# Eight edits to the order of a sliding-window attention and SwiGLU kernel: transposes of x 6 and 7, weights 10 and 11, scores 8 and 9

## The chip, the core and the metric

The kernel runs on one core of one Trainium2 chip. A core has five engines with instruction queues of their own: TensorE (PE in the profile; PEld is its weight load), VectorE (DVE), ScalarE (ACT), GpSimd (POOL) and SyncE (SP). [...] SP, ACT and POOL issue DMA transfers, which 16 DMA engines of the core carry out. The on-chip memory SBUF holds tiles of 128 partitions; TensorE writes to PSUM, eight banks of 128 x 512 float32, from which VectorE and ScalarE move the results on.

The metric is device time in microseconds, from one execution to another; 325.63 us is the median of three executions of the kernel before. Beside them there is one profiled execution, from which every row below comes.

## What is computed

Causal attention with a window of 64 positions over 8 batches, 8 heads, 576 positions and 64 features, and then, per token, a feed-forward block (512 to 1536 to 512) with a gate:

```python
scores = (1 / sqrt(64)) * q @ k.transpose(0, 1, 3, 2)
mask = (rel >= 0) & (rel < 64)  # rel: query position less key position
attn = softmax(where(mask, scores, -1e9))
x = (attn @ v).transpose(0, 2, 1, 3).reshape(B * S, H * D)
g = x @ w_gate
out = (g * sigmoid(g) * (x @ w_val)) @ w_out
```

Inputs and output are float32; the kernel computes in bfloat16 with sums in float32.

## The kernel before

The 4608 tokens are taken as 36 chunks of 128 for the attention, and as 9 blocks c of 512 for the feed-forward part, so that block c needs chunks 4c to 4c + 3. The program is written out as one list of operations in `build` (L1057). Each names the tiles that it reads and writes, and a small graph (L40 to L140) turns that into semaphore waits. The order of the list is the order in each engine's queue, and each queue runs strictly in that order. What follows names the parts that the change and the prediction touch.

Loads. `load` (L309) brings k, q or v of one chunk from DRAM and casts it; `load2(st)` (L327) brings k and q of two chunks, 2st and 2st + 1, into one of two row buffers (st modulo 2), so that load2(5) has to wait until the transposes of load2(3) have read theirs. `W(a, b)` (L994) brings the slices a to b - 1 of the gate weights and the value weights, 128 columns each. All of these are issued by POOL. `early_loads` (L1019), `more_loads`, `late_loads` and `next_loads` (L1040) group them; next_loads holds load2(5), k and q of 12 and 13 and v of 10 and 11.

Transposes of k and q. `T64(st)` (L371) transposes k and q of chunks 2st and 2st + 1 on TensorE, 64 instructions into two PSUM banks, and returns `ev(x, u, eng)`, which copies k or q of one of the two chunks to SBUF on the engine named. From chunk 12 on, `T` and `Tkq` (L360, L1053) do it by a DMA transpose on SP's queue.

Attention. `S2(n)` (L770) computes the scores of chunks n and n + 1: the products on TensorE, four exponentials on ACT, two masks on DVE. Scores of chunk n need k of n - 1 and n and q of n. `AVw(n)` (L625) multiplies with v for two chunks and divides by the sums; its last step on DVE (L661) writes x of the chunk, `xb`. `B2(n)` (L785) does scores n + 2, n + 3 and the values of n, n + 1 in one piece, in the steady part of the program.

Transposes of x. `X(n, eng)` (L797) brings xb of a chunk into xT, the operand of the feed-forward products. With eng "sp" it is one DMA transpose on SP's queue; with "act" or "dve" it is four transposes on TensorE into a bank and a copy by that engine (`Xp`, L810).

Feed-forward. `F(c, fs, lo, hi)` (L924) computes slices fs of the hidden layer for the tokens lo to hi of block c: four matmuls per slice with the gate weights, tanh on ACT, four per slice with the value weights, then two operations on DVE, `uu` (L902) and `hT` (L904). It takes either one slice for 512 tokens, which is 8 matmuls 512 wide, or two slices for 256 tokens, which is 16 matmuls 256 wide; both fill one bank for the gate and one for the value. `side` takes both banks as a neighbouring pair. `mid` runs something between the gate and the value matmuls. `lastF` is the last matmul group so far, and loads given it as a gate wait for that.

Output. `O(c, u, mid)` (L938) multiplies the hidden layer of 128 tokens of block c with w_out in 12 matmuls, slices 0 to 11 in order, copies the result on ACT and stores it; with `mid` it does nine matmuls, then mid, then three. Each group waits for all the hT slices that it reads before its first matmul. O2 copies on DVE, O3 does six and six.

The bank for a new piece of work is chosen when the list is written: the one, of those not held, whose last use stands furthest back in the list (L225).

Of the kernel before, what the change touches and what calls it, by code (L numbers as in the profile page):

```python
# [153 lines left out]
class _Kernel:  # L154
# [642 lines left out]
    def X(self, n, eng="sp", kind="f"):  # L797
        if n >= NCH:
            return
        g = self.g  # L800
        ix, it, u = n % 4, (n // 4) % self.NX, n % 4
        xb = self.xb[ix]
        xo = self.xT[it][:, :, 128 * u:128 * u + 128]
        xk = [("xb", ix, 0), ("xb", ix, 1)]
        if eng == "sp":
            g.op("sp", lambda e: e.dma_start_transpose(xo, xb[:, :]), reads=xk, writes=[("xT", it, u)], dma=True)
            return
        self.Xp(n, kind)(eng)
# [115 lines left out]
    def F(self, c, fs, lo=0, hi=512, mid=None, side=False):  # L924
        do = self.Fp(c, fs, lo, hi, side)
        for a in range(len(fs)):
            do("Wg", a)
        if mid:
            mid()
        do("tan", 0)  # L930
        for a in range(len(fs)):
            do("Wv", a)
        do("end", 0)
# [4 lines left out]
    def O(self, c, u, mid=None):  # L938
        io = (4 * c + u) % self.NO
        self.Omm(c, u, 0, 512, "act", [("ost", io), ("osth", io)], mid=mid)  # L940
        self.store(c, u)
# [77 lines left out]
    def early_loads(self):  # L1019
        self.load2(2)  # L1020
        self.W(8, 10)
        self.load(4, "v")
        self.load(5, "v")
        self.load2(3)
        self.W(10, 12)

    def more_loads(self):
        self.load_wo(0, 6)
# [28 lines left out]
    def build(self):  # L1057
        F, S, AV, X, O = self.F, self.S, self.AV, self.X, self.O
# [64 lines left out]
        ev = self.T64(2)  # L1123
# [3 lines left out]
        self.late_loads()  # L1127
        F(0, (7,))
        self.S2(4)
        F(0, (8,))  # L1130
        F(0, (9,), side=True)
        self.AVw(4)
        ev = self.T64(3)
        self.next_loads()
        for u in range(2):
            ev("k", u, "act")
            ev("q", u, "act")
        F(0, (10,))
        X(4, "act")
        F(0, (11,), mid=lambda: X(5, "act"))  # L1140
        F(1, (0, 1), 0, 256)
        self.S2(6)
        F(1, (2, 3), 0, 256)
# [2 lines left out]
        self.halves(7, "dve")  # L1146
        F(1, (4, 5), 0, 256)
        self.AVw(6)
        ev = self.T64(4)
        for u in range(2):  # L1150
            ev("k", u, "act")
            ev("q", u, "act")

        def mid():
            X(6, "act")
            X(7, "dve")

        O(0, 1, mid)
        F(1, (8,))
        self.init_kmask()  # L1160
        self.S2(8)
        ev = self.T64(5)
# [2 lines left out]
            ev("q", u, "act")  # L1165
        for n in (12, 13):
            self.Tkq(n)
        F(1, (9,))
        F(1, (0, 1), 256, 512)
        self.O2(0, 2)  # L1170
        self.B2(8)
# [1 line left out]
        X(8)  # L1173
        X(9)
        F(1, (2, 3), 256, 512)
        F(1, (6,))
        for n in (14, 15):
            self.load(n, "kq", self.lastF)
        F(1, (4, 5), 256, 512)
        self.O2(0, 3)  # L1180
        self.B2(10)
        self.store(0, 3)
        F(1, (7,))
        self.T(14, "k")
        X(10)
        X(11)
        self.T(14, "q")
        self.Tkq(15)
        F(1, (10,))
        F(1, (11,))  # L1190
        for n in (12, 13):
            self.load(n, "v", self.lastF)
        for n in (16, 17, 18):
# [84 lines left out]
```

## Time and profile before

| | us |
|---|---|
| median of three executions | 325.63 (324.99 to 326.03) |
| the profiled execution | 325.44 |
| its span, first to last instruction | 323.7 |
| granted TensorE clock | 1.0 of full speed |

| engine | busy us in the span |
|---|---|
| DVE | 218.7 |
| ACT | 127.1 |
| POOL | 104.3 |

A row of a timeline reads: start in us, us that it took, engine, line, operation, what it writes <- what it reads, sizes, how many were merged, and in brackets the idle time of the engine ahead of it and what ended that. An engine with a q behind its name is the sequencer issuing a DMA. In the chain of waits a row has start, us, engine, tile and line. A matmul's own duration in a timeline is longer than its step in a row of matmuls, because they overlap in the array; the chain and the distance of starts give the step. DMA rows give who issued, how many, their size and the median us from issue to landing.

The stretch that the change touches lies between about 27 and 80 us. Before it the kernel fills its pipeline, behind it the blocks 2 to 8 run in a steady order.

### The profile page before, as it was taken

To read this page: it belongs to the slowest core of one execution; us is meant where nothing else is said; L and a number is where in the kernel's file an instruction comes from. 1 tells how busy PE (TensorE), PEld (TensorE's weight loads), DVE (VectorE), ACT (ScalarE), POOL (GpSimd) and SP (SyncE) were. 2 spreads that over 40 slices of the span, in tenths; PEclk is the share of its full clock that TensorE was granted. 3 is DMA by queue.
4 is the path that set the end of the run, shared out by engine and by line. 5 is a ranking of instruction groups with operands and counts; after the bars stand their busy time and mean duration, and the time that the engine had idled before them with its cause. 6 is when DMAs were issued, how large, how long until landed. Compare 5 with 4: busy or idle time off the path is not lost.

```text
span 323.7 us, 7935 instructions
## 1 busy us (share of the span) xinstructions
PE 318.3 (98%) x3390; PEld 163.5 (51%) x3390; DVE 218.7 (68%) x407; ACT 127.1 (39%) x229; POOL 104.3 (32%) x135
## 2 busy tenths in 40 slices
PE   7999999999999999999999999999999999999996
PEld 5654575664545454545454544445454544444444
DVE  6788886678576976766767585858586767555510
ACT  3836656633433432433333332424242422222311
POOL 6998950042626071507060607060402000000000
PEclk9999999999999999999999999999999999999999
DMA  7999999999999699959996999999877202000012
GB/s 188 178 200 191 204 184 189 135 93 129 159 192 129 124 110 143 155 115 138 108 123 123 142 137 87 136 143 150 85 98 104 68 32 67 32 34 32 32 65 99
DMA packets 145219, 39.33 MB, mean 121 GB/s; under 512 B 130208, under 2 KB 140192, under 8 KB 145184
## 3 DMA queue, kind: packets, MB, share of 16 engines
q0 software_dynamic: 97936, 18.36, 69.6%
q1 hardware_dynamic: 41776, 10.63, 23.4%
q10 hardware_dynamic: 5472, 9.83, 9.2%
q8 instruction: 27, 0.44, 0.6%
q14 instruction: 8, 0.07, 0.1%
HBM read 37.75 MB, written 9.44 MB: 146 GB/s over the span
## 4 chain that ended last, share of the span: by engine, by line
PE 93%; POOL 2%; DVE 1%; DMA 1%; ACT 1%; issue 0%; ACTq 0%; POOLq 0%
PE ps L916 57%; PE ps L963 29%; PE ps L727 2%; PE ps L519 2%; DMA hT<-in_q_dram 1%; PE ps L469 1%; POOL vs L256 1%; PE ps L383 1%; ACT pt L481 1%; POOL va L325 1%; POOL Wv L345 0%; PE ps L819 0%; POOL Wg L345 0%; PE ps L473 0%; DVE uu L902 0%
## 5 line engine op out<-in xcount | busy, mean ns | idle before, releaser
L902 DVE SCALAR_TENSOR_TENSOR uu<-sig,ps 128x512 bf16<-128x512 bf16 x108 | 73.8, 683 | 55.9 <-ACT sig L897 55.9
L916 PE MATMUL ps<-xT,Wv 128*128 128x512 bf16 (+1 forms) x464 | 110.9, 364 | 0.3 <-DVE xb L661 0.3
L916 PE MATMUL ps<-xT,Wg 128*128 128x512 bf16 (+1 forms) x464 | 111.1, 365 | 0.0
L897 ACT ACTIVATE sig<-ps 128x512 bf16<-128x512 f32 x108 | 65.0, 603 | 86.7 <-PE ps L916 86.7
L963 PE MATMUL ps<-Wo,hT 128*128 128x512 bf16 (+1 forms) x444 | 98.8, 373 | 0.0
L904 DVE SCALAR_TENSOR_TENSOR hT<-uu,ps 128x512 bf16<-128x512 bf16 x108 | 74.2, 687 | 3.7
L916 PEld LDWEIGHTS ps<-xT,Wv 128*128 128x128 bf16 x464 | 45.3, 98 | 48.2 <-DVE xb L661 0.8
L963 PEld LDWEIGHTS ps<-Wo,hT 128*128 128x128 bf16 x444 | 43.3, 98 | 49.0
L916 PEld LDWEIGHTS ps<-xT,Wg 128*128 128x128 bf16 x464 | 43.6, 98 | 45.1 <-DVE xT L256 0.4
L325 POOL DMA_DIRECT2D kn<-in_k_dram x27 | 23.0, 855 | 113.2 <-PE ps L916 113.2
L325 POOL DMA_DIRECT2D va<-in_v_dram x40 | 34.1, 876 | 24.7 <-PE ps L916 24.7
L255 ACT ACTIVATE ost<-ps 128x512 f32<-128x512 f32 (+1 forms) x22 | 12.9, 588 | 52.9 <-PE ps L963 52.9
L256 DVE COPY ost<-ps 128x512 f32<-128x512 f32 (+1 forms) x15 | 10.1, 674 | 29.7 <-PE ps L963 29.6
L529 ACT ACTIVATE pt<-ps 128x512 bf16<-128x512 f32 x36 | 18.6, 602 | 29.0 <-PE ps L519 29.0
L325 POOL DMA_DIRECT2D qn<-in_q_dram x27 | 23.1, 861 | 2.1 <-DMA Wo<-in_moe_w_out_dram 2.1
L481 ACT ACTIVATE pt<-ps 128x512 bf16<-128x512 f32 x28 | 14.5, 602 | 14.1 <-PE ps L473 14.1
L762 DVE TENSOR_TENSOR xb<-ps,rc 128x512 bf16<-128x512 f32 (+2 forms) x39 | 18.8, 509 | 0.5
L727 PE MATMUL ps<-va,pt 64*64 64x65 bf16 x800 | 12.2, 192 | 0.0
L495 DVE TENSOR_TENSOR pt<-pt,kmask 128x1024 bf16<-128x1024 bf16 x18 | 11.5, 681 | 0.0
L727 PEld LDWEIGHTS ps<-va,pt 64*64 64x64 bf16 x800 | 10.3, 107 | 0.0
L495 DVE TENSOR_TENSOR pt<-pt,mask 128x1024 bf16<-128x1024 bf16 x14 | 9.3, 689 | 1.3 <-ACT pt L481 1.1
L758 DVE RECIPROCAL rc<-ps 128x8 f32<-128x8 f32 (+2 forms) x39 | 5.7, 174 | 6.4 <-PE ps L727 6.4
(76 smaller groups left out, 142.2 us busy)
## 6 DMA issues: line engine op xcount, KB each, us to landing
out_dram<-ost ACTq DMA_DIRECT2D x35, 256.0 KB, 3.0
va<-in_v_dram POOLq DMA_DIRECT2D x32, 128.0 KB, 5.1
kn<-in_k_dram POOLq DMA_DIRECT2D x21, 128.0 KB, 3.8
qn<-in_q_dram POOLq DMA_DIRECT2D x21, 128.0 KB, 4.5
Wv<-in_moe_w_val_dram POOLq DMA_DIRECT2D x6, 256.0 KB, 8.1
Wo<-in_moe_w_out_dram POOLq DMA_DIRECT2D x2, 768.0 KB, 17.7
Wg<-in_moe_w_gate_dram POOLq DMA_DIRECT2D x4, 256.0 KB, 7.8
ks<-in_k_dram POOLq DMA_DIRECT2D x3, 256.0 KB, 9.4
```

The lines of the kernel that those rows point to most:

```text
L256: return self.g.op(eng, lambda e: e.tensor_copy(d, a), reads=reads, writes=writes, after=after)
L325: self.g.op("pool", lambda e, d=d, a=a: e.dma_start(d, a), writes=ks, dma=True, after=gate)
L481: g.op("act", lambda e, po=po, p=p: e.activation(po, sv[p], ACTF.Exp, scale=SCALE), reads=[bx[p][1]], writes=[pk[p]])
L495: self.g.op("dve", lambda e: e.tensor_tensor(pt, pt, m, ALU.mult), reads=pk + mk, writes=pk)
L529: g.op("act", lambda e, po=po, p=p: e.activation(po, sv[p], ACTF.Exp, scale=SCALE), reads=[bx[p][1]], writes=[pk[p]])
L727: x = e.matmul(o, ab[0], ab[1], start=first, stop=phase == 1, skip_group_check=True)
L762: g.op("dve", lambda e, av=av, hs=hs, w=w, rc=rc, xo=xo: e.tensor_tensor(xo[:, :, hs, :], av[:, :, :, 0:64], rc[:, :, hs].unsqueeze(3).to_ ...
L897: g.op("act", lambda e: e.activation(sig[:, 0:w], G[:, 0:w], ACTF.Tanh, scale=0.5), reads=[gk], writes=[("sig", i)])
L902: g.op("dve", lambda e: e.scalar_tensor_tensor(uu[:, 0:w], sig[:, 0:w], 1.0, G[:, 0:w], ALU.add, ALU.mult), reads=[("sig", i), gk], writes ...
L904: g.op("dve", lambda e: e.scalar_tensor_tensor(out, v3(uu), 0.5, v3(V), ALU.mult, ALU.mult), reads=[("uu", i), vk], writes=[("hT", ih, f) ...
L916: r = e.matmul(bank[:, a * n:a * n + n], W[:, kk, f * 128:f * 128 + 128], xT[:, kk, lo:hi], start=(kk == 0), stop=(kk == NK - 1))
L963: r = e.matmul(OB[:, 0:n], hT[:, f, 128 * u:128 * u + 128], self.Wo[:, f, lo:hi], start=(f == 0), stop=(f == NF - 1))
```

## The change

It touches one method of loads and the middle of `build`. Weights 10 and 11 are loaded ahead of k and q of 6 and 7. F(0, 8) and F(0, 9) are done as two halves of the tokens, both slices at a time. T64(3) with its copies and next_loads goes from ahead of F(0, 10) to behind F(0, 11), and two of its four copies go from ACT to DVE. X(6) and X(7) become DMA transposes, issued ahead of T64(4); O(0, 1) runs in one piece. F(1, 6) to F(1, 11), one slice each for 512 tokens, become pairs of slices for 256 tokens each, the lower halves early and the upper halves in their old region, and S2(8) and T64(5) stand behind two lower halves, (6, 7) and (8, 9), where they stood behind F(1, 8).

```diff
@@ early_loads
         self.load(5, "v")
+        self.W(10, 12)
         self.load2(3)
-        self.W(10, 12)
@@ build
         F(0, (7,))
         self.S2(4)
-        F(0, (8,))
-        F(0, (9,), side=True)
+        F(0, (8, 9), 0, 256)
+        F(0, (8, 9), 256, 512, side=True)
         self.AVw(4)
-        ev = self.T64(3)
-        self.next_loads()
-        for u in range(2):
-            ev("k", u, "act")
-            ev("q", u, "act")
         F(0, (10,))
         X(4, "act")
         F(0, (11,), mid=lambda: X(5, "act"))
+        ev = self.T64(3)
+        self.next_loads()
+        for u, eng in enumerate(("act", "dve")):
+            ev("k", u, eng)
+            ev("q", u, eng)
         F(1, (0, 1), 0, 256)
         self.S2(6)
         F(1, (2, 3), 0, 256)
...
         F(1, (4, 5), 0, 256)
         self.AVw(6)
+        X(6)
+        X(7)
         ev = self.T64(4)
         for u in range(2):
             ev("k", u, "act")
             ev("q", u, "act")
-
-        def mid():
-            X(6, "act")
-            X(7, "dve")
-
-        O(0, 1, mid)
-        F(1, (8,))
+        O(0, 1)
+        F(1, (6, 7), 0, 256)
+        F(1, (8, 9), 0, 256)
         self.init_kmask()
         self.S2(8)
         ev = self.T64(5)
...
         for n in (12, 13):
             self.Tkq(n)
-        F(1, (9,))
+        F(1, (10, 11), 0, 256)
         F(1, (0, 1), 256, 512)
         self.O2(0, 2)
         self.B2(8)
...
         F(1, (2, 3), 256, 512)
-        F(1, (6,))
         for n in (14, 15):
             self.load(n, "kq", self.lastF)
         F(1, (4, 5), 256, 512)
         self.O2(0, 3)
         self.B2(10)
         self.store(0, 3)
-        F(1, (7,))
+        F(1, (6, 7), 256, 512)
         self.T(14, "k")
         X(10)
         X(11)
         self.T(14, "q")
         self.Tkq(15)
-        F(1, (10,))
-        F(1, (11,))
+        F(1, (8, 9), 256, 512)
+        F(1, (10, 11), 256, 512)
```

## The prediction

> **What bounds the kernel now.** I read the page first, then the chain that ended last in order of time, then the timeline of each engine in the stretch that the change touches.
>
> ```profile
> span 323.7 us, 7935 instructions
> PE 318.3 (98%) x3390; PEld 163.5 (51%) x3390; DVE 218.7 (68%) x407; ACT 127.1 (39%) x229; POOL 104.3 (32%) x135
> PE 93%; POOL 2%; DVE 1%; DMA 1%; ACT 1%; issue 0%; ACTq 0%; POOLq 0%
> ```
>
> TensorE is busy 318.3 of 323.7 us and makes 93% of the chain. So the change can only win TensorE work taken away or a TensorE wait removed, and it loses for each new wait of TensorE. In the chain by time the pieces from 36.63 on are TensorE's, one behind the other:
>
> ```profile
> 46.65 1.75 PE ps L916 x16
> ...
> 49.66 2.05 PE ps L963 x9
> 51.71 0.45 PE ps L819 x8
> 52.16 0.65 PE ps L963 x3
> 52.80 1.79 PE ps L916 x8
> ...
> 72.74 5.29 PE ps L916 x24
> ...
> 95.79 5.18 PE ps L916 x24
> ```
>
> These are prices: 24 matmuls 512 wide take 5.18 us (0.2158 each), 16 matmuls 256 wide 1.75 us (0.1094 each), and the eight transposes of x 6 and 7 inside O(0, 1) 0.45 us. The one TensorE wait of size in the touched stretch is in F(0, (10,)):
>
> ```profile
> 34.56 0.44 PE L383 MATMUL ps<-ident,ks 64*64 64x64 bf16 x32
> 35.30 1.02 PE L916 MATMUL ps<-xT,Wg 128*128 128x512 bf16 x4
> 36.63 1.02 PE L916 MATMUL ps<-xT,Wv 128*128 128x512 bf16 x4 [0.31 <-DVE xb L661]
> 37.49 0.39 PE L819 MATMUL ps<-ident,xb 128*128 128x128 bf16 x4
> 38.58 0.39 PE L819 MATMUL ps<-ident,xb 128*128 128x128 bf16 x4
> 42.14 1.05 PE L916 MATMUL ps<-xT,Wg 128*128 128x256 bf16 x8
> ```
>
> Four gate matmuls from 35.30 end at 36.16, and the value matmuls start at 36.63: 0.47 us lost. The row names VectorE's xb, but these matmuls read xT and Wv and write a bank that xb has no part in, so I look for a DMA that landed then:
>
> ```profile
> 22.70 0.71 POOL L335 DMA_DIRECT2D ks<-in_k_dram  x1
> 23.40 0.70 POOL L335 DMA_DIRECT2D qs<-in_q_dram  x1
> 24.09 0.77 POOL L345 DMA_DIRECT2D Wg<-in_moe_w_gate_dram  x1
> 24.84 0.76 POOL L345 DMA_DIRECT2D Wv<-in_moe_w_val_dram  x1
> ...
> qs<-in_q_dram POOLq DMA_DIRECT2D x1, 256.0 KB, 10.7
> Wg<-in_moe_w_gate_dram POOLq DMA_DIRECT2D x1, 256.0 KB, 11.1
> ```
>
> k and q of 6, 7 are issued ahead of weights 10, 11. qs landed at 23.40 + 10.7 = 34.1, Wg at 24.09 + 11.1 = 35.2. The trace has no landing for Wv, the next 256 KB of the same queue; one more step of 1.1 to 1.4 us gives 36.3 to 36.6 (estimate). So the wait was for Wv.
>
> **The change, part by part.**
>
> *Weights ahead, T64(3) later.* Wg and Wv take the queue places of ks and qs, so Wv lands near 34.1. F(0, (10,)) now follows AVw(4) directly, at 34.6, its value half at 35.5: the 0.47 us goes. ks and qs land by about 36.6 and are read at 38.9, so that is hidden. But the order behind it brings two other waits, and both are on VectorE:
>
> ```profile
> 35.85 0.69 DVE L661 TENSOR_TENSOR xb<-ps,rc 128x512 bf16<-128x512 f32 x1
> 41.45 0.68 DVE L902 SCALAR_TENSOR_TENSOR uu<-sig,ps 128x512 bf16<-128x512 bf16 x1
> ...
> 28.47 0.68 DVE L256 COPY kT<-ps 128x512 bf16<-128x512 bf16 x1
> 29.07 0.68 DVE L256 COPY qT<-ps 128x512 bf16<-128x512 bf16 x1
> ```
>
> First, xb of chunk 4 ends at 35.85 + 0.69 = 36.54, while F(0, (10,)) now ends at 34.61 + 1.73 = 36.34. X(4) waits until 36.60: 0.26 us. From there TensorE runs F(0, (11,)) with X(5) to 38.77, T64(3) 38.86 to 39.50 and F(1, (0, 1)) to 41.25. Second, two evictions of T64(3) are on VectorE now, queued behind uu and hT of F(0, (11,)). Before, X(5) ran at 38.58 and VectorE was ready for the next operation at 41.45. Now X(5) runs at 37.68, so the two copies (0.60 apart, 0.68 long) take that place at 40.55 and 41.15 and end at 41.83. S2(6) reaches the scores of chunk 7 at 41.62 and waits for q until 41.90: 0.28 us. Its end, where F(1, (2, 3)) follows, is 42.22 against 42.14 before. I take **+0.08 us** for this stretch (the 0.05 of the halved F(0, 8) and F(0, 9) is in it). If both waits were absent it would be -0.46; if each were 0.1 longer, +0.28.
>
> T64(3) also frees the buffers for load2(5), which GpSimd issued at 37.55 and now issues at 39.6. This is covered twice:
>
> ```profile
> 37.55 0.70 POOL L335 DMA_DIRECT2D ks<-in_k_dram  x1
> 44.85 0.68 POOL L325 DMA_DIRECT2D qn<-in_q_dram  x1 [2.09 <-DMA Wo<-in_moe_w_out_dram]
> ...
> va<-in_v_dram POOLq DMA_DIRECT2D x1, 128.0 KB, 13.4
> ```
>
> GpSimd waited 2.09 us for a Wo transfer a few issues later and has that slack, and v 9 ahead of it took 13.4 us to land, so the queue has work for far longer than 2 us. Cost nothing; without that cover T64(5) would be some 2 us late.
>
> *x 6, 7 by DMA.* **-0.45 us** for the eight transposes. The evictions went with a short wait of the matmuls behind them (1.79 against 1.73 for eight): **-0.06**. What it can cost is a late landing:
>
> ```profile
> 50.75 0.69 DVE L661 TENSOR_TENSOR xb<-ps,rc 128x512 bf16<-128x512 f32 x1
> 57.84 1.04 PE L916 MATMUL ps<-xT,Wg 128*128 128x256 bf16 x8
> ...
> kT<-kn SPq DMA_TRANSPOSE x2, 6.2
> qT<-qn SPq DMA_TRANSPOSE x2, 5.4
> ...
> DMA to landing us min/median/max: 2.4/3.4/7.3
> ```
>
> xb of 7 ends at 51.44, and X(7) goes out behind X(6) at about 51.9. Its first reader is the upper half of F(1, (0, 1)), at 57.84 before. Ahead of that stand three lower halves (5.25) instead of F(1, 8) and F(1, 9) (3.46), less 0.51, plus 0.08: 59.2 now. That leaves 7.3 us. The transposes of k and q 12, 13, issued in the same queue of loads a little later, took 5.4 to 6.2 (medians), the slowest of all 24 of k 7.3. So I take zero, with 0 to +1.0 us as bounds within 8 in 10 and a rival for the rest. On SP's queue Tkq(12) and Tkq(13) stand behind X(6) and X(7); they wait for their loads anyway and are read only in B2(10), near 71.
>
> *Halves.* The six F(1, 6 to 11) become 96 matmuls of 0.1094 in place of 48 of 0.2158: **+0.14 us**. [...]
>
> *Scores 8, 9 and T64(5) a step later.* They keep their order among themselves, and VectorE and ScalarE move with them: nothing, because F(1, (8, 9)) covers them as F(1, 8) did.
>
> *The order of the upper halves.* This is the wait that I find new. O(1, 0) reads hT 0 to 8 for its first nine matmuls. Before, F(1, (10,)) and F(1, (11,)) stood between F(1, (7,)) and O(1, 0). Now hT 8 is made by the last but one group:
>
> ```profile
> 77.73 0.69 DVE L904 SCALAR_TENSOR_TENSOR hT<-uu,ps 128x512 bf16<-128x512 bf16 x1
> 77.86 2.11 PE L963 MATMUL ps<-Wo,hT 128*128 128x512 bf16 x9
> ```
>
> VectorE is back to back there, behind the masks of B2(10), and ends its last but one hT at 77.73 + 0.69 = 78.42. TensorE would come to O(1, 0) at 77.86 + 0.07 (its share of the halves) and start at 78.48: **+0.55 us**. The number of VectorE operations since B2(10) is the same, so both ends move together. Bounds: 0, if VectorE runs ahead, to +0.7.
>
> *Sum.* 0.08 - 0.51 + 0.14 + 0.55 = +0.26 us. The profiled execution took 325.44 us (span 323.7 and 1.74 around it), so **325.7 us**; the median shown is 325.63, so this is no change. From there on the program is as before and TensorE has no wait to give back.
>
> **The rivals.**
>
> *X(7) lands late (slower).* SP's transposes could get hardly a turn while GpSimd's loads fill the DMA engines. For it is the first transpose of the kernel, k of 12:
>
> ```profile
> 54.27 1.29 SPq L368 DMA_TRANSPOSE kT<-kn  x1
> ...
> DMA to landing us min/median/max: 7.1/7.1/7.1
> ```
>
> It came in at 54.27 + 7.1 = 61.4. X(7), asked for 2.4 us earlier, meets more of the same loads; if it landed only with that one, TensorE would stand 2.2 us at the upper half of F(1, (0, 1)): 327.9 us. It decides from a time to landing over 7.3 us, and makes the kernel measurably slower above 8.2. Against it: no transpose of k took longer than 7.3, whatever loads stood beside it.
>
> *The new waits don't show (faster).* If VectorE is ahead at S2(6), X(4) and O(1, 0), the stretch gives -0.46 and O(1, 0) nothing: -0.46 - 0.51 + 0.14 = -0.83, 324.6 us. For it: each wait is under 0.6 us, less than one VectorE operation (0.69). Against it: VectorE's rows are back to back at all three places.
>
> *The wait at F(0, (10,)) stays.* If it were the bank or xb after all and not Wv, X(4) follows later by 0.2 and pushes S2(6): 0.2 to 0.3 more, 326.0 us. Against it: the code.
>
> **How the numbers follow.** My forecast has 0.63, the late X(7) 0.20, no new waits 0.10, the wait that stays 0.07. About 0.3%, 1 us, is what a measurement of this kernel can tell from no change (the three runs spread over 1.04 us). Slower by more than that needs X(7) 0.9 us late or more, or two waits at their upper bounds: 0.18 from the late X(7) and 0.08 from the upper ends of the others, 0.26. Faster needs nearly the whole -0.83 and more: 0.08. Same: 0.66. The terms' lower bounds give 324.6, the upper ones with 1.0 for X(7) 327.1; I take 324.7 to 327.0.
>
> **What would show it.** Right: no wait ahead of the value matmuls of F(0, (10,)); X(4) behind xb with a wait of about 0.25 us; S2(6) with one of about 0.3 ahead of its second half; O(1, 0) 0.5 us behind the matmuls ahead of it, put down to hT; no gap ahead of the upper half of F(1, (0, 1)); span near 324.0. Wrong: a gap of a microsecond or more there, put down to a transfer of xT, or TensorE without any of the three small gaps.

## The result, and the profile after

The changed kernel took 327.64 us in the median (327.14 to 329.44, 7 runs) against 325.74 us (324.99 to 326.16, 7 runs) for the kernel before on the same chip: a ratio of 1.0066, 95% interval 1.0043 to 1.009. It is slower by 1.9 us, clear of the noise, where the forecast was 325.7 us and the range ended at 327.0. The profiled execution took 327.21 us, 1.77 more than before's 325.44.

The head of the page after, the row of the queue that carries instructions, and the shares of the chain of waits:

```profile
span 325.5 us, 8012 instructions
PE 314.4 (97%) x3411; PEld 169.0 (52%) x3446; DVE 219.5 (67%) x408; ACT 125.6 (39%) x226; POOL 103.7 (32%) x135
q8 instruction: 27, 0.44, 0.6%
PE 89%; DVE 4%; POOL 2%; issue 2%; DMA 1%; ACT 1%; ACTq 0%; POOLq 0%
```

TensorE's share of the chain fell from 93% to 89%; VectorE (4%) and "issue" (2%), time in which the engine waited for nothing that the profile shows, took its place. A part of "issue" is only the place of the 35 matmuls that the trace lacks (3,446 weight loads, 3,411 matmuls). Where the rest is, the timeline of TensorE shows (start, duration, line, tiles, and in brackets the idle time before the row):

```profile
34.84 0.81 PE L916 MATMUL ps<-xT,Wg 128*128 128x512 bf16 x3 [0.16 <-issue]
35.48 1.03 PE L916 MATMUL ps<-xT,Wv 128*128 128x512 bf16 x4
36.74 0.40 PE L819 MATMUL ps<-ident,xb 128*128 128x128 bf16 x4 [0.23 <-DVE xb L661]
...
39.66 1.05 PE L916 MATMUL ps<-xT,Wg 128*128 128x256 bf16 x8
...
42.04 0.24 PE L469 MATMUL ps<-qT,kT 64*64 64x128 bf16 x2
...
43.63 0.24 PE L469 MATMUL ps<-qT,kT 64*64 64x128 bf16 x2 [1.21 <-issue]
43.63 0.25 PE L473 MATMUL ps<-qT,kT 64*64 64x64 bf16 x4
43.81 1.05 PE L916 MATMUL ps<-xT,Wg 128*128 128x256 bf16 x8
...
60.47 1.04 PE L916 MATMUL ps<-xT,Wg 128*128 128x256 bf16 x8
```

Down to 42.04 all goes nearly as forecast: no wait ahead of the value matmuls of F(0, (10,)) at 35.48, X(4) with a wait of 0.23 us for xb, the scores of chunk 7 with a short wait for q. (A "[0.16 <-issue]" ahead of three matmuls where four are due is a record that is missing, not a stop.) But in the middle of the scores of chunk 7 TensorE stands for 1.21 us, with all its inputs there, and F(1, (2, 3)) starts at 43.81 in place of 42.14. The last row is the upper half of F(1, (0, 1)), the first reader of X(7): it has no idle time before it.

The stop is in TensorE's weight loads too (first fence); in the kernel before, the same scores have none (second fence):

```profile
42.19 0.11 PEld L473 LDWEIGHTS ps<-qT,kT 64*64 64x64 bf16 x2
43.63 0.10 PEld L469 LDWEIGHTS ps<-qT,kT 64*64 64x64 bf16 x1 [1.32 <-issue]
```

```profile
41.92 0.22 PE L469 MATMUL ps<-qT,kT 64*64 64x128 bf16 x2
41.95 0.26 PE L473 MATMUL ps<-qT,kT 64*64 64x64 bf16 x6
```

The second loss is at O(1, 0). The list of TensorE's waits (total us, times, longest), its timeline and the chain by time have it:

```profile
PE ps L469 <- issue: 1.2, 1, 1.2
PE ps L963 <- DVE hT L904: 0.9, 2, 0.8
```

```profile
79.77 1.89 PE L963 MATMUL ps<-Wo,hT 128*128 128x512 bf16 x8 [0.76 <-DVE hT L904]
```

```profile
42.42 1.21 issue
...
78.80 0.70 DVE hT L904
79.50 0.27 issue
79.77 1.89 PE ps L963 x8
81.66 1.73 PE ps L916 x8
```

The last row is F(2, (0,)), at 79.97 before: 1.69 us late, and about that much is left at the end (span 325.5 against 323.7).

### The profile page after: what moved, and what is told of

It is laid out like the page before. It is cut to its first block, busy times and chain, and to the rows that moved or that the text cites. A ratio compares the mean times of both kernels' runs of the same rounds, so it can differ in the third digit from the quotient of the medians.

```text
span 325.5 us, 8012 instructions
## 1 busy us (share of the span) xinstructions
PE 314.4 (97%) x3411; PEld 169.0 (52%) x3446; DVE 219.5 (67%) x408; ACT 125.6 (39%) x226; POOL 103.7 (32%) x135
## 4 chain that ended last, share of the span: by engine, by line
PE 89%; DVE 4%; POOL 2%; issue 2%; DMA 1%; ACT 1%; ACTq 0%; POOLq 0%
PE ps L916 54%; PE ps L963 29%; PE ps L727 2%; PE ps L519 2%; DMA hT<-in_q_dram 1%; DVE uu L902 1%; PE ps L469 1%; DVE hT L904 1%; POOL vs L256 1%; POOL va L325 1%; POOL Wv L345 0%; PE ps L473 0%; POOL Wg L345 0%; DVE xb L762 0%; PE ps L383 0%
## 5 line engine op out<-in xcount | busy, mean ns | idle before, releaser
L916 PE MATMUL ps<-xT,Wv 128*128 128x512 bf16 (+1 forms) x484 | 110.5, 351 | 0.6
L916 PE MATMUL ps<-xT,Wg 128*128 128x512 bf16 (+1 forms) x481 | 107.9, 351 | 2.3 <-issue 2.2
L963 PE MATMUL ps<-Wo,hT 128*128 128x512 bf16 (+1 forms) x436 | 97.4, 373 | 1.2 <-DVE hT L904 0.9
L916 PEld LDWEIGHTS ps<-xT,Wv 128*128 128x128 bf16 x496 | 48.4, 98 | 44.6
L963 PEld LDWEIGHTS ps<-Wo,hT 128*128 128x128 bf16 x444 | 43.3, 98 | 49.8 <-DVE hT L904 0.8
L916 PEld LDWEIGHTS ps<-xT,Wg 128*128 128x128 bf16 x496 | 46.7, 98 | 42.2
L256 DVE COPY ost<-ps 128x512 f32<-128x512 f32 (+1 forms) x15 | 10.1, 673 | 29.2 <-PE ps L963 29.2
```

The costliest lines, as they stand in the source:

```text
L256: return self.g.op(eng, lambda e: e.tensor_copy(d, a), reads=reads, writes=writes, after=after)
L916: r = e.matmul(bank[:, a * n:a * n + n], W[:, kk, f * 128:f * 128 + 128], xT[:, kk, lo:hi], start=(kk == 0), stop=(kk == NK - 1))
L963: r = e.matmul(OB[:, 0:n], hT[:, f, 128 * u:128 * u + 128], self.Wo[:, f, lo:hi], start=(f == 0), stop=(f == NF - 1))
```

## The experiments

In every kernel with a changed warm-up two lines are added ahead, so that L916 of the profile before is L918 there, and L963 is L965. "Ratio" is to runs of the kernel before on the same chip.

The stop has no releaser. My guess was that TensorE waited for its own program. Counted in TensorE's compiled program (6,986 instructions of 64 bytes, 447,104 bytes; a weight load and a matmul are one each), the weight load that came late is instruction 1222 = 4 x 256 + 198. The kernel before has a small stop too, in the middle of the transposes of T64(5), at instruction 1733 = 6 x 256 + 197. And the row q8 above has 27 transfers with 0.44 MB, 16 KB each, which is nearly all of TensorE's program (the compiled programs of the other four engines have 7 to 35 KB). At 64 bytes each that makes a block of 256 instructions per transfer, an estimate from these sizes; the two stops lie 511 instructions apart, two such blocks less one. So theory A: TensorE ran out of its program. Rival B: the stop belongs to the scores of 7 in their new place. The way to tell them apart is to shift the whole program by some instructions that do nothing.

**Shift by 64.** The tiny matmuls go to a bank that nobody reads.

```diff
-    def warm(self, count):
+    def warm(self, count, pads):
...
+            for _ in range(pads):
+                r = e.matmul(bank[0:32, 0:16], self.wz[:, 0:32], self.wz[:, 0:16], start=True, stop=True)
...
-        self.warm(5)
+        self.warm(3, 36)
```

> The changed kernel with 64 more TensorE instructions ahead of its first transposes (two fp32 warm-up matmuls fewer, 36 tiny bf16 matmuls more, all into a bank that nobody reads); from there on the same instructions in the same order. Theory A (TensorE ran out of its own program: the profile has a queue named instruction with 27 transfers of 16 KB, 256 instructions each, and the stop of 1.21 us in the scores of chunk 7 stands at instruction 1222 = 4 x 256 + 198): the stop leaves that place, F(1, (2, 3)) starts 1.2 us earlier, near 42.6 in place of 43.81 us, the span falls from 325.5 to about 324.3 and the ratio to before from 1.0066 to about 1.003. Rival B (the stop belongs to the scores of chunk 7, by a wait that the new order brings): a stop of 1.2 us ahead of the same matmul, the same span of 325.5 and ratio 1.0066. In both, X(7) was just in time in the changed kernel; under theory A its reader comes 1.2 us earlier and part of the gain, up to 1.2 us, can go back into a wait there.

Ratio 1.0067 (1.0038 to 1.0095), span 325.1. The stop was gone, the time was not: the scores of chunk 7 ran through, but the timed runs gained nothing. Theory A was right on the stop and wrong on what it is worth. In the profile (326.79 us, the fastest of the nine runs) the reader of X(7) stood 0.5 us; the profile names nothing that ended this, but X(7), issued at 52.7, took 7.4 us to land, and the reader started at 60.12.

**The kernel before, shifted by 160.**

```diff
-        self.warm(5)
+        self.warm(1, 88)
```

> The kernel before, its order untouched, with 160 more TensorE instructions at its start (four fp32 warm-up matmuls fewer, 88 tiny matmuls more). Theory A: the places where a block of 256 instructions ends move by 160 instructions, into the two densest stretches of this kernel, T64(2) with F(0, (7,)) and S2(4) (256 instructions in about 3.7 us, where a fetch took 5.3 to 6.4 us) and S2(8) with T64(5): stops of about 1.6 us near the start of F(0, (8,)) and 1.8 us near F(1, (0, 1))'s upper half, and the 0.35 us stop in T64(5) goes; together 2.5 to 3.3 us slower than before, ratio 1.008 to 1.010. Rival B: the order is that of before, so no new stop, and the ratio is 1.000 within 0.002.

Ratio 1.0039 (1.002 to 1.0057), span 325.0. No stop of a microsecond came up: I had taken the time between two ends of blocks from their densest part alone (3.7 us), and the feed-forward matmuls in them stretch the two blocks to 4.5 us (28.84 to 33.34) and 6.1 us (56.20 to 62.30). What was slower was the start: with one warm-up matmul T64(2) began at 29.36 us in place of 27.27. A miss as a test of A, and a lesson for the later shifts.

**Eight matmuls of O(1, 0) ahead of F(2, (0,)).**

```diff
-            part(0, 9)
+            part(0, at)
...
-        O(1, 0, lambda: F(2, (0,)))
+        O(1, 0, lambda: F(2, (0,)), at=8)
```

> The changed kernel, with F(2, (0,)) put behind eight matmuls of O(1, 0) in place of nine, so that the first part reads hT 0 to 7 only. My theory of the second wait (O(1, 0) stands 0.7 to 0.8 us for VectorE's hT 8): the wait goes, F(2, (0,)) starts 0.8 us earlier less the 0.22 us matmul that moves behind it, and the end comes 0.7 to 0.8 us earlier: ratio to before near 1.004 in place of 1.0066. Rival: VectorE is the limit there, and the wait only moves, to F(2, (0,))'s value matmuls or to O's second part: ratio 1.0066 as it was, and the same 0.7 us put down to VectorE a line later.

Ratio 1.0041 (1.0019 to 1.0062): 0.8 us better than the change as it was, as expected. The wait for hT 8 was gone and nothing took its place. The stop in the scores of 7 was there again, at instruction 1222:

```profile
44.56 0.24 PE L469 MATMUL ps<-qT,kT 64*64 64x128 bf16 x2 [1.26 <-issue]
```

**Both.** The two edits above in one kernel.

> The shift by 64 instructions and the eight matmuls of O(1, 0) together. If the two waits are all that made the change slower, their gains add: 1.2 + 0.8 = 2.0 us under theory A, ratio to before near 1.000 (0.999 to 1.002); less by what X(7) then lets its reader wait. Rival B: the shift gives nothing, ratio 1.004 as for the eight matmuls alone.

Ratio 1.0024 (1.0011 to 1.0038), not 1.000. No stop, no wait for hT 8, but now a third one, put down to a transfer:

```profile
57.73 1.05 PE L918 MATMUL ps<-xT,Wg 128*128 128x256 bf16 x8
58.61 1.04 PE L918 MATMUL ps<-xT,Wv 128*128 128x256 bf16 x8
61.28 0.92 PE L918 MATMUL ps<-xT,Wg 128*128 128x256 bf16 x7 [1.63 <-DMA xT<-xb]
```

This is the late X(7) that the prediction had as a rival. In the changed kernel it had no wait only because TensorE had already lost 1.2 us. So there are three causes, and two of them overlap. How late X(7) is varies: in the four profiles of the changed kernel shifted by 12, 64 (two of them) and 40 instructions with the loads in their place its reader waits about 0.1, 0.5, 1.6 and 1.8 us.

**X(6), X(7) back on TensorE**, with the shift by 64 and the eight matmuls.

```diff
-        X(6)
-        X(7)
...
-        O(0, 1)
+
+        def mid():
+            X(6, "act")
+            X(7, "dve")
+
+        O(0, 1, mid)
```

> The shift by 64 instructions, the eight matmuls of O(1, 0), and x of chunks 6 and 7 transposed by TensorE again, in the middle of O(0, 1). Theory (three causes: TensorE out of its program, hT 8, and a landing of X(7) near 60 to 61 us that the first two hid): with all three taken away the change costs what I worked out for the rest; from the run of the shift with eight matmuls the wait for X(7) of 1.7 us goes and 0.5 us of transposes come back, ratio to before 0.999 to 1.002, no wait ahead of the upper half of F(1, (0, 1)). Rival: the wait there is not the landing of xT but something of the matmuls themselves; then it stays and the ratio is 1.004, 0.5 us above the run without it.

Ratio 1.0032 (1.0018 to 1.0046), between theory and rival. There was no wait for xT, so the rival's reason fell; but the profile began 1.5 us late. The mask matmuls at its start, here and in the changed kernel:

```profile
7.52 1.91 PE L425 MATMUL ps<-nmask,ident 128*128 128x512 bf16 x4
```

```profile
7.19 1.03 PE L425 MATMUL ps<-nmask,ident 128*128 128x512 bf16 x4
```

They took nearly twice as long, though the clock granted in that execution was 1.0. It was so in three of the five profiles with a shortened warm-up (the shift by 160, this one, and the next with all three repairs) and in none of the thirteen with all five warm-up matmuls. So the ratios of these kernels are probably too high by a part of that.

**Loads of k and q 12, 13 later**, alone and with the other two.

```diff
-        for n in (12, 13):
-            self.load(n, "kq")
...
         F(1, (6, 7), 0, 256)
+        for n in (12, 13):
+            self.load(n, "kq", self.lastF)
```

> The changed kernel with one edit: the four loads of k and q of chunks 12 and 13 on GpSimd's queue are issued behind F(1, (6, 7)) (and wait for it), some 9 us later than now, so that they no longer stand in the queue when X(6) and X(7) are issued. Theory (a transpose by DMA lands only when the loads asked for before it are through; X(7) had no wait in the changed kernel only because TensorE had stood 1.21 us before): X(7) lands 2 us earlier or more, near 57 us, but its reader comes at 60.4 us as now, so the ratio stays at 1.0066 (1.005 to 1.008) and the stop of 1.2 us in the scores of chunk 7 stays. Rival (X(7) was on the path already): the ratio falls by 0.002 or more. If the loads, now later, hold up the scores of chunk 12, a wait near 72 us shows it.

Ratio 1.0053 (1.0033 to 1.0072), inside what theory gave; the interval doesn't exclude a gain of 0.002. X(7), issued at 54.4 us, landed at 57.7; in the changed kernel it was issued at 53.6 and landed at 60.2, and nobody had waited for it. The stop was there, a little shorter, at instruction 1222:

```profile
44.24 0.24 PE L469 MATMUL ps<-qT,kT 64*64 64x128 bf16 x2 [0.84 <-issue]
```

> All three causes taken away, with x 6 and 7 left to the DMA: the shift by 64 instructions, the eight matmuls of O(1, 0), and the loads of k and q 12, 13 behind F(1, (6, 7)). Theory: X(6) and X(7) land some 5 us after their issue, near 57 us; no wait ahead of the upper half of F(1, (0, 1)); from the profile of the shift with eight matmuls 1.77 us go, so the end is 0.3 us ahead of before's: ratio 0.998 to 1.000. Rival (the landing is slow by itself, or TensorE's path has another wait): a wait of a microsecond or more stays there, ratio 1.002 to 1.004.

Ratio 1.0014 (0.9999 to 1.0029), with the slow start again (T64(2) at 29.15). None of the three waits was left in the profile.

**The change without its first part**: T64(3), its copies, the weights' place and F(0, 8), F(0, 9) as before.

```diff
         self.AVw(4)
+        ev = self.T64(3)
+        self.next_loads()
+        for u in range(2):
+            ev("k", u, "act")
+            ev("q", u, "act")
...
-        ev = self.T64(3)
-        self.next_loads()
-        for u, eng in enumerate(("act", "dve")):
-            ev("k", u, eng)
-            ev("q", u, eng)
```

> The change without its first part: weights 10, 11 behind k and q 6, 7, T64(3) ahead of F(0, (10,)), its copies on ScalarE and F(0, 8), F(0, 9) whole, all as before; the rest as in the changed kernel. Theory of three causes: no stop in the scores of chunk 7 (the 256 instructions of a block no longer fall into one dense stretch), F(1, (2, 3)) at 42.1 us as before; the reader of X(7) comes near 58.5 us, X(7) lands at 60 to 61, so 1.5 to 2.5 us of wait there, and 0.5 to 0.8 us for hT 8: ratio 1.004 to 1.008, no better than the whole change. Rival (the move of T64(3) is what made it slower, and X(7) is in time): the 1.67 us go, ratio 1.001 to 1.002.

Ratio 1.0041 (1.0023 to 1.0059): slower than before by more than the rival allows. The stop was gone, the wait for hT 8 was there; the wait for X(7) was 0.46 us in the profiled run, less than the 1.5 that I had expected. The profile gives no releaser for that wait either; X(7) landed just ahead of its end, at 59.8. Undoing the part with the stop gives back 0.8 us (0.0025 in the ratios, whose intervals overlap) of the 1.67 that this part had lost.

**A shift with a warm start.** All five warm-up matmuls stay and 20 tiny ones (40 instructions) stand behind them.

```diff
-        self.warm(5)
+        self.warm(5, 20)
```

> A cleaner shift: all fp32 warm-up matmuls stay, 20 tiny matmuls (40 instructions) behind them, in time in which TensorE waits for k and q anyway. The earlier shift had taken two warm-up matmuls away, and in two of the profiles with it the first matmuls ran at half speed (1.91 us for four in place of 1.03), about 1.5 us late from the start. Theory: the stop of 1.21 us in the scores of chunk 7 goes (the boundary of its block moves to the first matmuls of F(0, (10,)), 2 us earlier), and about 1.0 us of it comes back as a wait for X(7), so the ratio falls from 1.0066 to 1.004 to 1.006 only. Rival (with a warm start nothing comes back): 1.0025.

Ratio 1.0061 (1.0043 to 1.0079), the upper edge of what theory gave. The scores of chunk 7 end at once, and F(1, (2, 3)) starts at 42.64:

```profile
42.45 0.22 PE L469 MATMUL ps<-qT,kT 64*64 64x128 bf16 x2
42.48 0.23 PE L473 MATMUL ps<-qT,kT 64*64 64x64 bf16 x4
42.64 1.05 PE L918 MATMUL ps<-xT,Wg 128*128 128x256 bf16 x8
```

The chain by time (start, duration) shows where the gain went, from the issue of X(7) to its reader:

```profile
52.47 8.71 DMA xT<-xb
61.18 0.09 issue
61.27 0.81 PE ps L918 x6
```

Of 1.17 us won at F(1, (2, 3)), nothing is left at 61.27, where the changed kernel was at 60.47. The wait is 1.81 us by the timeline.

**The shift by 40 with the eight matmuls and the late loads.**

> The cleaner shift by 40 instructions, the eight matmuls of O(1, 0), and the loads of k and q 12, 13 behind F(1, (6, 7)). Theory: no stop in the scores of 7, no wait for X(7), no wait for hT 8; from T64(2) to the end of the stretch 0.3 to 0.8 us less than before, ratio 0.997 to 1.000. Rival (something else in the change costs, that the late start of the earlier run with 1.0014 has hidden or caused): 1.001 or more.

Ratio 0.999 (0.998 to 1.0001), as expected. TensorE no longer waits for X(7). In the DMA activity from 54 to 56 us (packets, MB, share of 16 engines), first with the loads in their place (the shift by 40 alone), then with the loads later:

```profile
q0 software_dynamic: 2237, 0.28, 222.7%
q1 hardware_dynamic: 81, 0.02, 7.8%
```

```profile
q1 hardware_dynamic: 743, 0.18, 57.5%
q0 software_dynamic: 165, 0.02, 16.1%
```

and the median us to landing in the stretch from 50 to 60, in the same order:

```profile
xT<-xb SPq DMA_TRANSPOSE x2, 8.6
```

```profile
xT<-xb SPq DMA_TRANSPOSE x2, 4.6
```

q0 carries GpSimd's loads, q1 the transposes: in the kernel before q0 moved 12,505 packets from 10 to 40 us, where GpSimd alone issues, and q1 none; from 54 to 60, with the four transposes of k and q 12, 13, q1 moved 1,061. In the first of the two kernels here q1 had moved no packet from 50 to 54 and 81 by 56, though X(6) was issued at 51.1; q0, with the loads asked for before it, moved 4,924 from 50 to 56.

**The shift by 40 with the eight matmuls, and x 6, 7 on TensorE.**

> The cleaner shift, the eight matmuls of O(1, 0), and x 6 and 7 transposed by TensorE. Theory: 0.5 us more than with the DMA and the late loads, ratio 0.999 to 1.001; no wait for a transfer. Rival: the same as with the earlier shift, 1.003.

Ratio 1.001 (0.9994 to 1.0025): the three waits away, by the other way. X(6), X(7) on TensorE cost 0.45 us more (325.99 against 325.54) than by DMA with the loads out of the way, as much as their eight transposes take; the two intervals overlap.

**X(4) in the middle of F(0, (11,))**, on top of the version with late loads.

```diff
-        X(4, "act")
-        F(0, (11,), mid=lambda: X(5, "act"))
+        F(0, (11,), mid=lambda: X(4, "act"))
+        X(5, "act")
         ev = self.T64(3)
```

> The version with the cleaner shift, eight matmuls and late loads, and X(4) in the middle of F(0, (11,)) with X(5) behind it, in place of X(4) ahead of F(0, (11,)) with X(5) in its middle. Theory: the wait of X(4) for VectorE's xb (0.23 us in the changed kernel, 0.3 to 0.5 in the runs since) goes and nothing takes its place, since T64(3) covers the copy of X(5): 0.3 us less than without this edit, ratio 0.996 to 0.999. Rival: F(1, (0, 1)) then waits for ScalarE's copy of X(5), up to 0.6 us: the same or 0.3 us more.

Ratio 0.9983 (0.9973 to 0.9994): faster than before. The wait for xb is gone.

**Does the shift alone do anything?** The kernel before with `warm(5, 20)`.

> The kernel before with the 20 tiny matmuls behind the warm-up and nothing else: a control for the shift by 40. Theory: the added matmuls cost nothing (TensorE waits there for k and q), and in this order the boundaries of the program's blocks fall where 256 instructions last longer than a fetch, but for the small stop of 0.25 to 0.35 us in T64(5), which stays about as it is: ratio 1.000 (0.998 to 1.002). Rival (the shift by itself makes any order faster or slower): the gain of the version with late loads and X(4) in the middle, 0.0017, or more shows here too, 0.998 or less.

Ratio 0.9984 (0.9973 to 0.9994), on the edge of the rival. Its profile has a span of 323.8 us, no less than before's 323.7, so the gain isn't in the order of the work that it shows. But it has the best proof of A. TensorE's weight loads, first before, then the control:

```profile
55.85 0.21 PEld L383 LDWEIGHTS ps<-ident,qs 64*64 64x64 bf16 x16 [0.25 <-issue]
```

```profile
55.71 0.11 PEld L383 LDWEIGHTS ps<-ident,ks 64*64 64x64 bf16 x4 [0.43 <-issue]
```

The small stop in T64(5) moved from the middle of q's transposes into k's, 40 instructions earlier in the work, and stayed at instruction 1733 of the program.

**A shift by 12**, with `warm(5, 6)`.

> The changed kernel with 6 tiny matmuls (12 instructions) behind the warm-up. Theory of the fetch: in three profiles the stop ended 5.3 to 5.7 us after TensorE had passed the end of the block before (instruction 966). With 12 more instructions ahead that end lies 0.8 us earlier, ahead of the gates of F(0, (11,)) in place of its values, and the block after it begins 12 instructions earlier in the scores of chunk 7, 0.03 to 0.1 us. So the stop is again at instruction 1222 = 4 x 256 + 198 of the program, six matmuls earlier in the work, and lasts 0.3 to 0.7 us in place of 1.2. Rival (the stop belongs to one place of the work, or is the same length wherever it falls): 1.2 us, or ahead of the same matmul as in the changed kernel.

326.29 us in one run, span 324.6. There was no stop at all; both theories had one. The rows of the last scores of 7 and of what follows:

```profile
42.67 0.22 PE L469 MATMUL ps<-qT,kT 64*64 64x128 bf16 x2
42.69 0.23 PE L473 MATMUL ps<-qT,kT 64*64 64x64 bf16 x4
42.85 1.05 PE L918 MATMUL ps<-xT,Wg 128*128 128x256 bf16 x8
```

The transfers of the instruction queue say why there was none, not what sets them off. In the three kernels with the stop the one that matters began at 41.2, 42.1 and 42.0 us (changed kernel, eight matmuls, late loads alone), about 3.2 us behind instruction 966. In this kernel it began at 38.5, 0.9 us behind that instruction, and with a shift by 40 at 38.3. So a transfer does not come at a fixed time after one instruction has run; X(4)'s wait for VectorE lies 12 instructions ahead of 966 here, 24 in the changed kernel. What the transfers do show is what ends a stop. Take the n-th transfer as the block that begins at about instruction 198 + 256 n: then in the changed kernel the block from 1222 had arrived at 42.21 us, just as TensorE ran out at 42.20, and TensorE went on at 43.63, 1.42 us later. In the five other profiles with one of the two stops it went on 1.25 to 1.56 us behind the end of that transfer, and in none of the eighteen profiles did it begin a block sooner than 1.25 us behind it.

**Repaired version and control side by side.**

> The repaired version (20 tiny matmuls behind the warm-up, eight matmuls of O(1, 0), late loads of k and q 12, 13, X(4) in the middle of F(0, (11,))) again, on one chip with the control. The first time it stood at 0.9983, and the control, the kernel before with the same tiny matmuls, at 0.9984, each beside its own runs of the kernel before. Theory (the repaired change is worth something of its own: from T64(2) to the scores of chunk 12 its profile has 58.2 us, the control's 59.2): 0.5 us or more below the control on the same chip, ratio 0.996 to 0.998. Rival (the whole gain is that of the tiny matmuls, and a late start is made up in either kernel): the same as the control within 0.3 us.

> The control, the kernel before with the 20 tiny matmuls, again, beside the repaired version on one chip. Theory: 0.998 to 1.000, and 0.5 us or more above the repaired version. Rival: the same as the repaired version within 0.3 us.

The repaired version: 324.92 us, ratio 0.9964 (0.9942 to 0.9986). The control: 325.36 us, 0.9988 (0.9965 to 1.001). The repaired version beats the kernel before. Against the control it is 0.44 us ahead in the medians, between the 0.5 of theory and the 0.3 of the rival, with overlapping intervals of the two ratios. The spans of the profiles differ by more, 322.7 against 323.8, but a span alone proves little: the same repaired version had 323.7 in its first profile, where T64(2) began at 28.13 us in place of 27.25. From T64(2) to the end the repaired version has 295.45 and 295.59 us in its two profiles, the control 296.36 in both, the kernel before 296.45; some 0.8 to 0.9 us is what the repaired order saves in them. The first row is the page's, the next two TensorE's waits, of the repaired version:

```profile
span 322.7 us, 8053 instructions
...
PE ps L918 <- issue: 2.2, 14, 0.2
PE ps L875 <- DVE wz L259: 1.4, 1, 1.4
```

No wait of the touched stretch is left among the long ones (the 14 times 0.2 us are places of missing records).

## Why the prediction was wrong

*The step that failed* is "I take +0.08 us for this stretch", from Wv's wait to F(1, (2, 3)). It was +1.67: 43.81 against 42.14. The parts that it had were right: Wv's wait gone, X(4) with a wait of 0.23 us (0.26 forecast), the scores of 7 held by VectorE's copy of q (0.28 forecast, about 0.3 measured). Those scores began at 42.04 and not at 41.90, because xb of chunk 4 ended at 36.68 and not at 36.54; that is 0.14 of the miss of 1.59. The rest, 1.45 us, is a wait for TensorE's own program, which the sum did not have: from the start of one weight load to the next it is 1.43 us (42.20 to 43.63), of which the timeline counts 1.21 as idle time of the matmuls. Moving T64(3) put its 128 short instructions directly ahead of F(1, (0, 1)) (32) and S2(6) (96), and a block's end fell into the scores of 7: the 256 instructions from 966 to 1222 went in 4.2 us (38.01 to 42.20), and TensorE got on with the next block only 5.6 us after 966. With the shift by 40 the same block lasts 7.0 us (34.97 to 41.95), and nothing stops. The length alone does not decide, though: a block of 4.5 us ran without a stop in the kernel shifted by 160, and one of 6.1 us ended in the small stop of the kernel before. That it was the program is shown: the stop sat at instruction 1222 in three kernels with the same start, left with a shift of 12, 40 or 64 instructions and no change in the order of the work, the other one stayed at instruction 1733 when the work moved by 40, and each ended behind a transfer of the instruction queue. What sets the time of a transfer is open.

*X(7).* "I take zero" held in the trace, for a wrong reason: not because 7.3 us were enough, but because the stop had moved its reader to 60.47; X(7) came at 60.20. That was luck. The rival that X(7) lands late was right in mechanism: with the stop gone, TensorE stood 1.81 us there in the shift by 40 (2.2 in the rival). That this kernel took 327.76 us, next to the rival's 327.9, is in part luck again: the shift by 12 waited only 0.1 us there. The prices of other transposes, medians of 5.4 to 6.2, did not carry over, since the loads of 12 and 13 were still in the queue when X(6) went out. With these loads issued 13 us later (54.97 against 41.66) it was 4.6.

*O(1, 0).* Right in mechanism, a little small in size: a wait of 0.76 us for hT 8 against 0.55, put down to VectorE, and given back by taking one matmul from the first part.

*x 6, 7 off TensorE and the halves.* From 43.81 to F(2, (0,)) at 81.66 are 37.85 us, against 37.83 from 42.14 to 79.97 before. The steps' -0.51 and +0.14 with 0.76 for hT 8 make +0.39, and +0.02 was measured; 0.35 of the difference is before's small stop in T64(5) (55.51 to 55.85 from one weight load to the next), which was gone. It was in the trace of before (0.25 us of idle time) and I had passed over it: the one sign there that TensorE can stop without a releaser.

*load2(5), S2(8) and T64(5)* cost nothing, as said. "Faster" at 0.08 and the wait that stays at F(0, (10,)) did not come.

In sum +0.26 was forecast and +1.77 measured. Of the 1.51 between them 1.59 are from the first stretch, 0.21 from hT 8, -0.35 from T64(5); 0.06 stay unassigned. The range left too little room above, because the late X(7) was the only large loss that it knew.

## What to carry to other kernels

Before moving short matmuls together, look for stops put down to nothing in the trace of before, and count where they lie in the engine's program; a few idle instructions ahead tell a stop of the program from one of the data (here the stop of 1.21 us left with 12, 40 and 64 of them). A move to DMA was priced here by what stood in the queues at the time of its issue (8.6 us to landing with the loads of 12 and 13 ahead of it, 4.6 with them later), not by the medians of other transposes (5.4 to 6.2). And where two waits lie one behind the other, taking away the first shows the second: the shift alone measured as nothing here (1.0067 and 1.0061 against 1.0066), all repairs together as 0.9983 and 0.9964. The kernel before with the same shift has 0.9984 and 0.9988, so not all of that gain is the repairs'.

## What the hardware showed that was not expected

- TensorE stood 1.21 us inside a dense stretch for a block of its program: 27 transfers of 16 KB in the whole run, stops at 4 x 256 + 198 and 6 x 256 + 197. At nearly all ends of blocks nothing of it shows, but it does where a block lasted 4.2 us, and in T64(5) of the kernel before, where it lasted 6.1 us. TensorE went on 1.25 to 1.56 us behind the end of the transfer.
- With three of five warm-up matmuls the first mask matmuls took 1.91 us in place of 1.03 in two of four profiles, and T64(2) began at 28.9 and 29.2 us there, at 27.4 and 27.5 in the other two.
- The control with 20 tiny matmuls behind the warm-up measured 0.9984 and 0.9988, though its profiles show nothing shorter (the second interval, 0.9965 to 1.001, includes no change). Why is open.
- In the shift by 40, while GpSimd's loads moved 2,237 packets from 54 to 56 us, SyncE's queue, with X(6) and X(7) issued at 51.1 and 52.5, moved 81.
